# A gated linear recurrence and an ELU layer on one core: loads merged and spread over three queues, one table set for Ln and Exp, and the hand-written order replaced

## The chip, the core and the metric

The kernel runs on one core of a Trainium2 chip. A core has five engines that run side by side and meet only at semaphores: TensorE (PE; its weight loads are listed apart as PEld), VectorE (DVE), ScalarE (ACT), GpSimd (POOL) and SyncE (SP), which here only issues transfers. Each engine carries out its own list of instructions strictly in order. Transfers are issued by an engine into a queue of that engine and are then carried out by the DMA engines.

The metric is the time of one execution on the device in microseconds, the median of three runs.

## What is computed

The inputs are q, k, v, a_re and a_im of 4 batches, 8 heads, 768 steps and 48 values a head, and two weight matrices, `w_in` (384 x 2048) and `w_out` (2048 x 384), which arrive in double precision. Cut to what matters:

```python
mag = np.sqrt(a_re * a_re + a_im * a_im)
scale = np.minimum(mag, 0.999) / (mag + 1e-06)
a_re_n, a_im_n = (a_re * scale, a_im * scale)
for t in range(S):
    new_re = ar * S_re - ai * S_im
    new_im = ar * S_im + ai * S_re
    kv = np.einsum('bhd,bhe->bhde', k[:, :, t], v[:, :, t])
    S_re, S_im = (new_re + kv, new_im)
    y[:, :, t] = np.einsum('bhd,bhde->bhe', q[:, :, t], S_re)
...
h = x @ w_in
g = np.where(h > 0.0, h, alpha * (np.exp(np.minimum(h, 0.0)) - 1.0))
return g @ w_out
```

The complex gate `a` decays and turns a 48 x 48 state for each head; the outputs of the heads side by side, 3072 rows of 384, go through the two matrix products with an ELU between them.

## The kernel before

**Units.** The work is cut into 12 units (`NU`). A unit is 128 steps of two batches (`NB = 2`, function `where`): even units are batches 0 and 1, odd units batches 2 and 3, and each pair of units takes the next 128 steps. For a unit, `load` brings `ar`, `ai`, `q`, `k` and `v`, with one transfer for each of the two batches, that is 128 x 8 runs of 192 bytes, 192 KB. All go through SyncE's queue.

**One unit's steps.** Squares (`squared`, `squares`, ACT) are added (`joined`: for unit 0 on TensorE, otherwise on DVE or POOL); `logarithms` and `powers` (ACT, Ln and Exp) give the length of the gate and its inverse, `lengths`, `ratios`, `slopes` (DVE) the decay and the tangent, `angles` (ACT, arctangent) the angle. Products with triangular matrices on TensorE sum decays and angles over the steps (`sums`, `summed`, `decays`, `turned`), ACT takes exponentials (`decayed`, `quarters_used`) and sine and cosine (`waves`), DVE scales and gates q and k (`scaled`, `gated`). `noted` checks that the gate lies in the range for which this way is exact; `carry_on` keeps the last angle for the next unit of the pair. `ends` spreads the decay at chunk ends. Then the gated q and k are transposed (TensorE into PSUM, ACT copies back, L1024), `scores` and `states` are formed, `values` gives the outputs, ACT copies them out, and `seam` moves 16 rows of each head pair into place by small transfers.

**The layer.** For a unit, `inner` (L1210) forms two of 16 blocks of h, `elu` takes Relu and Exp on ACT and one `scalar_tensor_tensor` on DVE (L1221), `project` (L1235) multiplies with `w_out`. There are three PSUM buffers for `inner`, so a block waits for the `elu` of the third before. From unit 2 on the two products are cut down with sums of submatrices (`product`, L1319; `mult`, L1455), which need more additions on DVE and sums of the weights prepared once (`summed_in`, `combined`).

**Weights.** `fetch` brings one of 8 parts of `w_in` or of `w_out` (768 KB each). A part of `w_in` comes in four transfers: 48 rows into partitions 0 to 47, 48 into 64 to 111, and two of 16 rows into the gaps. `convert` rounds a part to single precision in five DVE operations, one a call (L40, L43, L46, L50, L655). Only then may `inner` or `project` use it.

**Order.** The order is written out by hand for the first 200 us or so, in the list `first`, and after that comes from `plan`: functions with a due time each, sorted. The program is issued to each engine in this order; what a transfer may overwrite is held back by semaphores. A table of activation functions is chosen with `preload_act_table_set` (`table`), and further loads stand where a function needs another set. Before, Ln comes from the set `natural_log` and Exp from `exp_and_others`; sine, cosine and arctangent from `trig_and_small`.

Lines that the prediction names: L598 load of a unit, L644 part of the weights, L705, L709, L710 squares, L716 `joined`, L731, L735, L736 logarithms, L742, L746, L747 powers, L772 lengths, L791 `noted`, L811 and L815 angles, L837 turned, L889 the first product of the decays, L920 and L904 exponentials, L951 and L954 `ends`, L973 and L977 waves, L1003 gated, L1077 to L1081 states, L1190 seam.

Of the kernel before, what the change touches and what calls it, by code (L numbers as in the profile page):

```python
# [16 lines left out]
C = 128  # L17
# [3 lines left out]
LEAST_RE = 0.7  # L21
# [484 lines left out]
def kernel(  # L506
# [12 lines left out]
    nc = tc.nc  # L519
    B, H, S, D = q.shape  # L520
# [3 lines left out]
    HD = H * D  # L524
    NB = 2
# [56 lines left out]
    def load(u, name, src, bufs, pad=False):  # L582
# [11 lines left out]
        for n in range(NB):  # L594
            to = t[:, n]
            if pad:
                to = to[:, 0:HD].rearrange("p (h d) -> p h d", h=H)
            nc.sync.dma_start(  # L598
                out=to, in_=src[b + n, :, ds(s, C)].rearrange("h p d -> p h d")
            )  # L600
        nat[u][name] = t

    def load_a(u):
        load(u, "ar", a_re, 1)
        load(u, "ai", a_im, 1)

    def load_qk(u):
        load(u, "q", q, 1)
        load(u, "k", k, 1)

    def load_v(u):
        load(u, "v", v, 2, pad=True)
# [28 lines left out]
    def fetch(kind, m):  # L641
        t, dst, pairs = weights_of(kind, m)
        for to, of in pairs:
            nc.sync.dma_start(out=to, in_=of)  # L644
        raw[kind, m] = t, dst
# [869 lines left out]
    load_a(0)  # L1515
    nc.scalar.preload_act_table_set("natural_log")
# [61 lines left out]
    def gates_of(u, *at):  # L1578
# [7 lines left out]
        (load_qk, 0), (squared, "ar", 0), (load_v, 0), (squared, "ar", 1), (squared, "ai", 0),  # L1586
        (joined, 0, 0), (squared, "ai", 1), (joined, 0, 1), (logarithms, 0, 0), (logarithms, 0, 1),
        (fetch, "in", 1), (fetch, "in", 2), (ratios, 0, 0), (lengths, 0, 0), (warm, 2), (warm, 1),
        (lengths, 0, 1), (sums, 1), *2 * [(convert,)], (table, "exp_and_others"), (ratios, 0, 1),
        (powers, 0, 0), (powers, 0, 1), (warm, 2), (sums, 0), (warm, 1), (angles, 0, 0),  # L1590
        (angles, 0, 1), (summed, 0), (summed, 1), (decayed, 0, 0), (turned, 0, 0), (decayed, 0, 1),
        (turned, 0, 1), (waves, 0, 0), (waves, 0, 1), (begun, 1), (scaled, 0, "q", 0), (warm, 1),
        (scaled, 0, "k", 1), (scaled, 0, "k", 0), (ends, 0), (scaled, 0, "q", 1), (warm, 1),
        (noted, 0), (convert,), (gated, 0, 0), (warm, 1), (warm, 2), (gated, 0, 1), (warm, 2),
        (convert,), (transposed, 0, "q", 0), (convert,), (transposed, 0, "k", 0),
# [179 lines left out]
```

## Time and profile before

| | us |
|---|---|
| median of three runs (667.33 to 667.91) | 667.35 |
| the profiled execution | 665.7 |
| its span, first to last instruction | 663.7 |
| TensorE busy | 640.6 (97%) |
| VectorE busy | 501.9 (76%) |
| ScalarE busy | 418.9 (63%) |
| GpSimd busy | 153.8 (23%) |
| L40, L43, L46, L50, L655: one operation on 128 x 768 | 0.557, 0.955, 0.556, 0.954, 0.956 |
| L1221: one operation on 128 x 512 | 0.681 |
| a table load | 1.28 |

The span is what the profile sees of one execution. Busy time is an average over stages that have different limits, so it has to be read by stretches. A matmul is listed as two instructions and its end is modelled, so a busy TensorE isn't TensorE at its peak: blocks of L1210 follow each other at 2.6 us when nothing holds them. In the chain of waits a line gives start, duration and what was under way; "issue" is time in which the engine waited for nothing that the profile shows, and "SPq" is SyncE issuing a transfer. The idle time before an instruction is put down to the semaphore that came last.

### The profile page before, as it was taken

How to read it: one execution, taken by the hardware profiler on the slowest of the kernel's cores; microseconds unless marked ns; L12 is line 12 of the kernel's file. 1: busy time of each engine (PE TensorE's matmuls, PEld its weight loads, DVE VectorE, ACT ScalarE, POOL GpSimd, SP SyncE). 2: the span in 40 equal slices, each digit the busy share in tenths (PEclk: the TensorE clock that was granted, in tenths of full speed). 3: DMA queues.
4: the chain of work that ended last, by engine and by line, in shares of the span. 5: the costliest groups of instructions: out<-in, count | busy, mean ns of one | idle time of the engine just before them, and what ended most of it. 6: DMA issues, size and time to landing. Idle time of an engine off the chain costs nothing.

```text
span 663.7 us, 17229 instructions
## 1 busy us (share of the span) xinstructions
PE 640.6 (97%) x7236; PEld 580.2 (87%) x7236; DVE 501.9 (76%) x801; ACT 418.9 (63%) x684; POOL 153.8 (23%) x200
## 2 busy tenths in 40 slices
PE   8889999999999899999999999999999999999995
PEld 6868886576897898998998998998998999999995
DVE  5798999967868689578678678678668768764481
ACT  6885367586756566767667667667677677571250
POOL 2000000112124313413403503503503502402000
PEclk9799999999999999999999999999999999999999
DMA  9997745732800713333442442451451551212100
GB/s 164 178 146 117 150 143 155 131 74 48 128 2 16 136 35 85 80 84 80 77 93 72 78 99 62 83 106 50 93 105 46 100 105 44 53 33 61 35 2 30
DMA packets 151443, 56.12 MB, mean 85 GB/s; under 512 B 129684, under 2 KB 143164, under 8 KB 151356
## 3 DMA queue, kind: packets, MB, share of 16 engines
q1 hardware_dynamic: 147616, 53.58, 39.8%
q0 software_dynamic: 3520, 1.20, 1.6%
q8 instruction: 59, 0.97, 0.6%
q14 instruction: 28, 0.23, 0.1%
q10 hardware_dynamic: 220, 0.14, 0.1%
HBM read 48.91 MB, written 4.80 MB: 81 GB/s over the span
## 4 chain that ended last, share of the span: by engine, by line
PE 63%; DVE 14%; ACT 10%; issue 5%; DMA 4%; SPq 3%; DVEq 0%; ACTq 0%
PE mlp L1319 20%; PE mlp L1455 10%; PE mlp L1210 7%; PE y L1455 5%; PE w L1023 4%; DVE g L1471 4%; PE mlp L1235 3%; PE y L1235 3%; PE y L1109 3%; DVE g L1480 3%; SPq L598 3%; DMA w<-in_moe_w_in_dram 3%; PE w L1064 2%; PE w L837 2%; ACT ee L1477 2%
## 5 line engine op out<-in xcount | busy, mean ns | idle before, releaser
L1319 PE MATMUL mlp<-w_out,g 128*128 128x192 f32 x640 | 111.8, 328 | 1.0 <-DVE ee L1331 1.0
L1319 PEld LDWEIGHTS mlp<-w_out,g 128*128 128x128 f32 x640 | 104.2, 190 | 4.4 <-DVE ee L1331 1.6
L1081 POOL TENSOR_TENSOR S<-S,T 128x384 f32<-128x384 f32 x36 | 30.2, 839 | 174.0 <-DVE S L1079 174.0
L1210 PE MATMUL mlp<-x,w_in 128*128 128x256 f32 x288 | 65.1, 384 | 0.2
L1210 PEld LDWEIGHTS mlp<-x,w_in 128*128 128x128 f32 x288 | 54.7, 193 | 9.2 <-DVE g L1221 0.7
L1471 DVE TENSOR_TENSOR g<-g,mlp 128x512 f32<-128x512 f32 x45 | 30.6, 681 | 40.1 <-ACT qt L1024 28.6
L1297 DVE TENSOR_TENSOR g<-g 128x512 f32<-128x512 f32 x80 | 54.4, 694 | 5.0 <-PE mlp L1319 3.8
L1455 PE MATMUL mlp<-x,w_in 128*128 128x128 f32 x424 | 56.2, 275 | 0.4 <-DVE o L1344 0.4
L1480 DVE SCALAR_TENSOR_TENSOR g<-ee,g 128x512 f32<-128x512 f32 x63 | 47.5, 754 | 11.1 <-ACT ee L1477 11.0
L1319 PE MATMUL mlp<-w,g 128*128 128x192 f32 x320 | 54.5, 329 | 0.0
L1319 PEld LDWEIGHTS mlp<-w,g 128*128 128x128 f32 x320 | 51.8, 190 | 0.6
L1455 PEld LDWEIGHTS mlp<-x,w_in 128*128 128x128 f32 x424 | 51.6, 192 | 0.7 <-DVE o L1344 0.6
L1190 POOL DMA_DIRECT2D x<-y x62 | 29.9, 489 | 94.8 <-ACT y L1126 43.5
L1476 ACT ACTIVATE ee<-g 128x512 f32<-128x512 f32 x63 | 39.5, 627 | 17.4 <-DVE g L1471 17.0
L1468 ACT COPY g<-mlp 128x512 f32<-128x512 f32 x36 | 21.1, 585 | 43.9 <-PE mlp L1455 43.7
L1477 ACT ACTIVATE ee<-ee 128x512 f32<-128x512 f32 x72 | 45.4, 631 | 2.3
L1024 ACT COPY qt<-w 128x512 f32<-128x512 f32 x48 | 25.8, 591 | 15.6 <-PE w L1023 15.4
L904 ACT ACTIVATE n<-w 64x384 f32<-64x384 f32 (+1 forms) x60 | 28.1, 486 | 8.9 <-PE w L889 8.3
L973 ACT ACTIVATE cs<-n 128x768 f32<-128x768 f32 (+1 forms) x14 | 10.5, 751 | 35.7 <-DVE n L845 35.6
L1455 PE MATMUL mlp<-x,g 128*128 128x128 f32 x224 | 29.7, 275 | 1.2 <-DVE o L1344 1.2
L1079 DVE TENSOR_TENSOR S<-w,S 128x384 f32<-128x384 f32 x38 | 21.0, 553 | 12.2 <-POOL S L1081 10.0
L1455 PE MATMUL y<-x,w_in 128*128 128x128 f32 x216 | 29.0, 277 | 1.2 <-ACT g L1468 1.2
(222 smaller groups left out, 1428.7 us busy)
## 6 DMA issues: line engine op xcount, KB each, us to landing
w<-in_moe_w_out_dram SPq DMA_DIRECT2D x8, 768.0 KB
g<-in_moe_w_in_dram SPq DMA_DIRECT2D x24, 256.0 KB
g<-in_moe_w_out_dram SPq DMA_DIRECT2D x24, 256.0 KB
w<-in_moe_w_in_dram SPq DMA_DIRECT2D x16, 288.0 KB
vn<-in_v_dram SPq DMA_DIRECT2D x24, 192.0 KB
ar<-in_a_re_dram SPq DMA_DIRECT2D x22, 192.0 KB
ai<-in_a_im_dram SPq DMA_DIRECT2D x22, 192.0 KB
q<-in_q_dram SPq DMA_DIRECT2D x22, 192.0 KB
```

The source lines that it names most:

```text
L904: nc.scalar.activation(out=flat(x[key][to, n : n + 1]), in_=t[of], func=AF.Exp, scale=sign)
L1081: eng.tensor_tensor(out=new_s, in0=new_s, in1=wide, op=ALU.mult)
L1190: eng.dma_start(out=x["x"][ds(j * HP + D, G), i], in_=x["y"][ds(j * HP + i * G, G)])
L1210: nc.tensor.matmul(t[:, e], lhsT=w_in[:, i, ts(f + e, C)], rhs=x["x"][:, i], start=(i == 0), stop=(i == NI - 1),)
L1235: nc.tensor.matmul(x["o", n], lhsT=x["g", f // 8][:, f % 8, ts(n, C)], rhs=w_out[:, f], start=(f == 0), stop=(f == NF - 1),)
L1297: nc.vector.tensor_tensor(out=S_of(u, k, h), in0=a, in1=b, op=op)
L1319: nc.tensor.matmul(to, lhsT=a[:, m], rhs=b[:, m], start=(first and h == 0 and m == 0), stop=False, skip_group_check=True,)
L1455: nc.tensor.matmul(x["c" + c][:, ts(m, C)], lhsT=a[:, m], rhs=x["mix"][p], start=(p == BANKS[c][0] and m == 0), stop=False, skip_group_che ...
L1471: nc.vector.tensor_tensor(out=part(u, to), in0=part(u, a), in1=part(u, b), op=op)
L1476: nc.scalar.activation(out=e, in_=part(u, of), func=AF.Relu, scale=-1.0)
L1477: nc.scalar.activation(out=e, in_=e, func=AF.Exp, scale=-1.0)
L1480: nc.vector.scalar_tensor_tensor(out=part(u, to), in0=nat[u]["e", to], scalar=-1.0, in1=part(u, of), op0=ALU.add, op1=ALU.max,)
```

## The change

- `load` brings both batches of a tensor in one transfer of 128 x 16 runs of 192 bytes, except v (its rows are padded) and unit 0's ar and ai.
- `brought` loads one tensor of a unit, by SyncE or, with `second`, by ScalarE. ScalarE issues unit 0's ai, k and q and unit 1's ar and ai.
- `fetch` gives every second transfer of a part of `w_in` to GpSimd: SyncE brings rows 0 to 47 and the first gap, GpSimd the other half. A part of `w_out` is one transfer and stays with SyncE.
- Ln and Exp both come from the set `natural_log_exp_and_others`.
- The bound of the check, `LEAST_RE`, is 0.7072 instead of 0.7.
- The list `first` is another one: unit 1's squares, logarithms and powers stand ahead of much of unit 0's states; unit 2's q and k are fetched before parts 1 and 2 of `w_in`; the check `noted` of unit 0 comes after the first half of unit 1; blocks of the layer come in another order. The plan behind the list is the same but for the name of the table.

```diff
-LEAST_RE = 0.7
+LEAST_RE = 0.7072
...
-    def load(u, name, src, bufs, pad=False):
+    def load(u, name, src, bufs, eng, pad=False):
...
-        for n in range(NB):
-            to = t[:, n]
-            if pad:
-                to = to[:, 0:HD].rearrange("p (h d) -> p h d", h=H)
-            nc.sync.dma_start(
-                out=to, in_=src[b + n, :, ds(s, C)].rearrange("h p d -> p h d")
+        if pad or u == 0 and name in ("ar", "ai"):
+            for n in range(NB):
+                to = t[:, n]
+                if pad:
+                    to = to[:, 0:HD].rearrange("p (h d) -> p h d", h=H)
+                eng.dma_start(
+                    out=to, in_=src[b + n, :, ds(s, C)].rearrange("h p d -> p h d")
+                )
+        else:
+            eng.dma_start(
+                out=t.rearrange("p n h d -> p (n h) d"),
+                in_=src[ds(b, NB), :, ds(s, C)].rearrange("n h p d -> p (n h) d"),
             )
         nat[u][name] = t
 
+    def brought(u, name, second=False):
+        src = {"ar": a_re, "ai": a_im, "q": q, "k": k, "v": v}[name]
+        load(u, name, src, 1, nc.scalar if second else nc.sync, pad=name == "v")
+
     def load_a(u):
-        load(u, "ar", a_re, 1)
-        load(u, "ai", a_im, 1)
+        brought(u, "ar")
+        brought(u, "ai")
...
-        for to, of in pairs:
-            nc.sync.dma_start(out=to, in_=of)
+        for n, (to, of) in enumerate(pairs):
+            (nc.gpsimd if n % 2 else nc.sync).dma_start(out=to, in_=of)
...
-    load_a(0)
-    nc.scalar.preload_act_table_set("natural_log")
+    brought(0, "ar")
+    brought(0, "ai", True)
+    nc.scalar.preload_act_table_set("natural_log_exp_and_others")
...
-        (load_qk, 0), (squared, "ar", 0), (load_v, 0), (squared, "ar", 1), (squared, "ai", 0),
-        (joined, 0, 0), (squared, "ai", 1), (joined, 0, 1), (logarithms, 0, 0), (logarithms, 0, 1),
-        (fetch, "in", 1), (fetch, "in", 2), (ratios, 0, 0), (lengths, 0, 0), (warm, 2), (warm, 1),
-        (lengths, 0, 1), (sums, 1), *2 * [(convert,)], (table, "exp_and_others"), (ratios, 0, 1),
...
+        (squared, "ar", 0), (squared, "ai", 0), (brought, 0, "v", False), (squared, "ar", 1),
+        (brought, 0, "k", True), (brought, 0, "q", True), (squared, "ai", 1), (joined, 0, 0),
+        (logarithms, 0, 0), (lengths, 0, 0), (joined, 0, 1), (brought, 1, "ar", True),
+        (logarithms, 0, 1), (lengths, 0, 1), (ratios, 0, 0), (ratios, 0, 1), (warm, 2), (sums, 0),
+        (sums, 1), (convert,), (powers, 0, 0), (warm, 1), (powers, 0, 1), (convert,),
+        (table, "trig_and_small", 0), (summed, 0), (angles, 0, 0), (summed, 1), (angles, 0, 1),
+        (decayed, 0, 1), (decayed, 0, 0), (turned, 0, 0), (turned, 0, 1), (brought, 1, "ai", True),
+        (waves, 0, 0), (scaled, 0, "k", 0), (begun, 1), (convert,), (waves, 0, 1),
+        (scaled, 0, "k", 1), (ends, 0), (warm, 2), (warm, 1), (warm, 1), (scaled, 0, "q", 0),
+        (load_qk, 2), (table, "natural_log_exp_and_others", 0), (scaled, 0, "q", 1), (warm, 1),
+        (gated, 0, 0), (warm, 1), (gated, 0, 1), (carry_on, 0), (fetch, "in", 1), (convert,),
+        (fetch, "in", 2), (squares, 1), (transposed, 0, "q", 0), (warm, 2), (transposed, 0, "k", 0),
+        (joined, 1), (convert,), (states, 0, 0), (logarithms, 1), (scores, 0, 0), (powers, 1),
+        (transposed, 0, "q", 1), (warm, 2), (transposed, 0, "k", 1), (ratios, 1), (lengths, 1),
+        (values, 0, 0), (slopes, 1), (scores, 0, 1), *4 * [(convert,)], (brought, 1, "q", False),
+        (decays, 1), (warm, 2), (states, 0, 1), (angles, 1), (warm, 2), (brought, 1, "k", False),
+        (values, 0, 1), (seam, 0), (fetch, "in", 3), (convert,), (turns, 1), (ends, 1), (convert,),
+        (table, "trig_and_small", 1), (noted, 1), (warm, 1), (waves, 1), (scaled, 1), (gated, 1, 0),
+        *2 * [(convert,)], (brought, 1, "v", False), (load_a, 2), (convert,), (warm, 4),
+        (inner, 0, 2), (gated, 1, 1), (fetch, "in", 4), (convert,),
+        (table, "natural_log_exp_and_others", 1), (transposed, 1, "q", 0), (transposed, 1, "k", 0),
+        (warm, 2), (states, 1, 0), (scores, 1, 0), (inner, 0, 0), (noted, 0), (load_v, 2),
+        *3 * [(convert,)], (fetch, "in", 5), (transposed, 1, "q", 1), (convert,),
+        (transposed, 1, "k", 1), (convert,), (values, 1, 0), (scores, 1, 1), (inner, 0, 4),
+        *4 * [(convert,)], (elu, 0, 2), (states, 1, 1), (convert,), (elu, 0, 0), *2 * [(convert,)],
+        (elu, 0, 4), (convert,), (values, 1, 1), (inner, 0, 6), (convert,), (inner, 0, 8),
...
-                put(r + (19.45 if u < PAIRED + 4 else 21.1), table, "exp_and_others", u)
+                put(r + (19.45 if u < PAIRED + 4 else 21.1), table, "natural_log_exp_and_others", u)
```

## The prediction

> **What bounds the kernel now.** First the busy time by stretch (stretch, length, then busy time and instruction count of PE, PEld, DVE, ACT and POOL, granted clock, DMA share, GB/s):
>
> ```profile
> 10.00:20.00 10.00, 7.21 (x54) 5.05 (x54) 6.54 (x14) 9.90 (x15) 0.64 (x1) 0.96 1.31 184
> 50.00:60.00 10.00, 10.00 (x69) 8.86 (x69) 9.63 (x13) 5.42 (x9) 0.49 (x1) 1.00 0.84 138
> 90.00:100.00 10.00, 10.00 (x48) 8.80 (x47) 9.76 (x14) 6.17 (x10) 0.00 (x0) 1.00 0.48 156
> 240.00:400.00 160.00, 158.41 (x2126) 150.80 (x2126) 122.12 (x206) 109.93 (x177) 52.48 (x57) 1.00 0.36 78
> ```
>
> Three regimes: to 25 us ScalarE's chain and the DMA engines (share over 1); from 25 to 125 us VectorE, which rounds the weights; from 75 us to the end TensorE. What remains for TensorE after about 200 us is the same list of work in both kernels, so a change there counts only where TensorE stands idle. The largest wait of TensorE between 200 and 600 us (total, times, longest):
>
> ```profile
> PE w L889 <- DVE n L772: 2.0, 8, 0.2
> ```
>
> It is 0.24 us, once a unit. The chain of waits says what is ahead of it (start, us, what):
>
> ```profile
> 298.58 1.28 ACT L735
> 299.86 0.01 issue
> 299.87 0.84 ACT n L735
> 300.71 0.73 ACT n L736
> 301.45 0.02 issue
> 301.46 0.04 ACT L746
> 301.50 1.26 issue
> 302.76 0.94 ACT n L746
> 303.70 0.02 issue
> 303.73 0.97 DVE n L772
> 304.69 0.04 issue
> 304.74 0.88 PE w L889 x8
> ```
>
> The first line is a table load for Ln (L735), the 1.26 us "issue" another for Exp (L746): 2.56 us of a chain that makes TensorE wait 0.24. At the start ACT's timeline shows the same, and the chain shows SyncE held while it issues loads:
>
> ```profile
> 9.31 0.49 ACT L731 ACTIVATE n<-w 128x384 f32<-128x384 f32 x1 [0.80 <-PE w L720]
> 9.81 1.28 ACT L1200 ACT_TABLE_LOAD   x1
> ...
> 20.09 0.60 ACT L977 ACTIVATE cs<-cs,quarter 128x384 f32<-128x384 f32 x1
> ```
>
> ```profile
> 7.45 3.90 SPq L598
> ...
> 22.14 4.38 SPq L598
> ```
>
> An issue otherwise takes 0.38 to 0.56 us. When the 3.90 ends at 11.35, SyncE had handed over 2.16 MB (ar, ai, a w_in part, q, half of k); at the 186 GB/s that the stretch 2:16 shows from 2 us on, 1.74 MB were moved. At the end of the 4.38 the sum is 4.91 against 4.41 MB. So a queue holds some 0.42 to 0.50 MB of 192-byte runs, and then the issuing engine waits.
>
> **The Trainium skill.** "ScalarE: Activation LUTs", What ACT_TABLE_LOAD costs, gives about 1283 ns for a load and as much again for a drain; the trace agrees on 1.28 and shows the chain resuming within 0.02 us, so I count 1.28. The same page, Table sets, says that natural_log_exp_and_others holds both functions. "DMA: Bandwidth & Descriptors", Issuing engines are not separate DMA queues, says that the queues of three engines run on the same 16 DMA engines and that spreading saves only issue time; the trace has one busy queue, so it cannot contradict. I share the bandwidth equally among queues.
>
> **The change, part by part.**
>
> *One table set.* From unit 3 on, Ln and Exp of a unit stand next to each other, and both loads before L735 and L746 go; each unit keeps two loads. Nine waits of 0.24 to 0.25 us (eight in 200:600, one at 199.59) end at L772, which comes up to 2.56 us earlier: 9 x 0.24 = 2.2. Bounds: nothing, if another releaser is as late; 2.2, since TensorE is otherwise busy. I take 2.1. Loads removed between 97 and 200 us lie under TensorE's products, which are busy 20.0 of 20 us there: nothing, and up to 1.28 each if that cover is gone.
>
> *ScalarE issues loads.* Before, ACT ran squares, logarithm 0, logarithm 1 (ended 9.80). Now, in order: two issues of ai, three squares, k, q, the last square, logarithm 0, unit 1's ar, logarithm 1. Each of the last three loads is a merged transfer of 2048 runs (0.39 MB). k fits. q is held until k has mostly drained, ar until q has; behind them stand the last square and logarithm 1. When ar's issue ends, ACT's queue has drained 4 x 0.39 - 0.46 = 1.11 MB; at equal shares SyncE drained about as much (ar, half a w_in part, v: 1.18) and GpSimd its 0.39: 2.68 MB. At 186 GB/s that is 14.4 us after 2.0; at 200, an estimate[...], 13.4. Taken: 15.4, then logarithm 1 ends at 15.9. If no issue is held (0.45 each) it is 11.3; at 170 GB/s 18.2.
>
> From there: lengths, the second power (+1.15), no table load (before 1.28), one load (1.28), two arctangents (0.94): +3.4, 19.3; the turns on TensorE +0.6; then VectorE's own row of turns, scaling and gating, 15.07 to 24.95 before, unchanged work 9.9. Gating of unit 0 ends at 29.8, 4.85 us later than before.
>
> *SyncE and GpSimd.* Unit 2's q and k now stand on SyncE ahead of w_in parts 1 and 2 and wait until unit 0's are gated. Their 0.79 MB, then half of part 1 (0.39), from 30 us: landed near 38, and VectorE wants part 1 at about 39.5, after unit 1's slopes. GpSimd's halves of parts 1 and 2 stand behind unit 0's carry, so from 24 us on; nothing of the seam is late for them. Part 4's half on SyncE stands behind unit 2's ar, which waits for the check of unit 0 (L791) on ACT, now put behind unit 1's first transposes: it lands about 0.5 us after VectorE wants it. The gain in issue time on SyncE is nothing by itself: it was on no engine's path but through data.
>
> *The remade list.* VectorE from the end of gating (24.87) to unit 1's last state (72.06) was 47.2 us, of which idle 1.66 + 0.79 + 0.50 + 1.15 + 0.37 = 4.5: work 42.7. The new order has, up to the same state, three rounding instructions less (L655, L40, L43: 2.3) and one less L1221 (0.6): 39.8. New idle: 0.8 behind TensorE's broadcast of the ends, 0.5 for part 4, 0.4 for others: 1.7. So 29.8 + 39.8 + 1.7 = 71.3, and unit 1's values end on TensorE near 70.8. TensorE then runs dense. Before, it had four L1210 blocks behind it at 72.2 (and lost another 0.6 up to 101); now three, so break-even is 72.2 + 0.6 - 2.6 = 70.2. Loss 0.6. In the dense stretch blocks of 2.6 us take turns with a rounding (4.0) and an L1221 (0.6) on VectorE; summed up by those rows from the last state on, the sixth and ninth L1221 come 0.2 and 0.6 us after TensorE wants their buffers, and the last part of w_out 0.9 after its product: about 1.7 in all. Before, TensorE lost 1.1 at 141 to 145, behind copies of transpositions (the new order puts products between these), beside the 0.6 already counted. Difference taken as zero, bounds -1 and +2.
>
> Sum: -2.1 + 0.6 = -1.5. The profiled execution took 665.7 us (span 663.7); against its time 664.2, against the median 667.35 **665.8 us**. The execution shown is 1.65 below the median, which I treat as the same offset in both kernels.
>
> **Rivals.**
> 1. *Slower: unit 1's ai comes late.* ACT squares it ahead of unit 0's transposition copies (L1024). It is issued after the exponentials, near 22.5, and competes with 0.79 MB of w_in from GpSimd; at 186 GB/s shared it lands between 27.5 and 32. ACT reaches it at 28.1, and each us later moves copies, scores and states, that is VectorE, by one. At 32 the sum is -1.5 + 4 = +2.5: 669.9. It decides from a landing at 31.0 on. For it: the share over 1 in 10:20, 2-KB runs against 192-byte runs; against it: GpSimd's halves may themselves wait for the carry.
> 2. *Faster: ACT isn't held*, because its queue has more room than SyncE's or drains first. Logarithm 1 then ends at 11.3, all is 4.6 us earlier: 661.2. For it: no issue by ACT was held before (0.50 us each); against it: the 3.90 and the 4.38.
> 3. *No change: the dense stretch is less well fitted*, a rounded part of w_out is late for its product by 1.5 us more: 667.3. For it: VectorE is 9.76 of 10 us busy there; against it: the work is the same.
>
> **How the numbers follow.** My sum 0.40, rival 1 0.32, rival 2 0.18, rival 3 0.10. The likeliest case alone reaches from 664 to 667.5. 0.2% (1.3 us) is about what a measurement of this kernel can tell from no change; the likeliest lies close to that edge, 0.24 of its 0.40 beyond it. Faster 0.24 + 0.18 = 0.42; same 0.16 + 0.07 + 0.01 = 0.24; slower 0.31 + 0.03 = 0.34. The range for eight in ten runs from rival 2's time to a little past rival 1's: 661 to 670.5.
>
> **What would show it.** Tables: the wait of L899 (the old L889) for VectorE gone from TensorE's waits after 200 us; if it still totals 2 us, that step is wrong. The hold: issues of q and ar by ACT of several us between 8 and 16; if they take 0.5, rival 2. The start: second half of unit 0's gating ending near 29.8, the last state of unit 1 near 71. Rival 1: ACT idle ahead of its second whole square (L720) with ai's load as releaser. Rival 3: TensorE idle between 72 and 140 us with L665 as releaser. What makes all of it wrong is a data wait on VectorE that I put at no cost: part 1 has only 1.5 us to spare.

## The result and the profile after

The changed kernel takes 671.3 us in the median (670.88 to 672.33), the kernel before 667.33 in the same session (665.58 to 667.91). The ratio is 1.0066, with a 95% interval of 1.0052 to 1.0080: slower, where the forecast said 665.8 and faster. The profiled execution took 671.3 us, its span is 669.6 (before: 665.7 and 663.7), so that the two traces differ by more (5.6 us) than the medians (4.0).

First the stretches that the prediction showed (stretch, length, then busy time and instruction count of PE, PEld, DVE, ACT and POOL, granted clock, DMA share, GB/s):

```profile
10.00:20.00 10.00, 5.50 (x13) 3.69 (x14) 3.08 (x6) 4.68 (x9) 0.00 (x0) 0.68 1.29 169
50.00:60.00 10.00, 9.74 (x126) 8.80 (x128) 9.33 (x14) 7.88 (x16) 2.02 (x4) 0.83 0.91 149
90.00:100.00 10.00, 10.00 (x48) 8.81 (x47) 9.65 (x14) 4.92 (x8) 0.00 (x0) 1.00 0.48 145
240.00:400.00 160.00, 159.18 (x1998) 152.51 (x1997) 122.62 (x206) 105.19 (x176) 49.96 (x54) 1.00 0.41 83
```

Behind 240 us TensorE is busy for 0.77 us more in 160 us than before, and its only waits from 200 to 600 us (total, times, longest) are others than the one of 2.0 us for L772:

```profile
PE mlp L1465 <- DVE o L1354: 1.7, 2, 1.2
PE y L1465 <- ACT g L1478: 1.3, 1, 1.3
PE w L1074 <- DVE S L1089: 0.4, 1, 0.4
```

Where the chain of the kernel before held two table loads, ScalarE's timeline now has the four activations (the old L735, L736, L746, L747) back to back:

```profile
257.25 0.85 ACT L745 ACTIVATE n<-ar 128x768 f32<-128x768 f32 x1
257.99 0.83 ACT L746 ACTIVATE n<-n 128x768 f32<-128x768 f32 x1
258.86 0.94 ACT L756 ACTIVATE n<-n,ln_eps 128x768 f32<-128x768 f32 x1
259.70 0.83 ACT L757 ACTIVATE n<-n 128x768 f32<-128x768 f32 x1
```

So the loss stands in the first 80 us: VectorE ends the last state of unit 1 at 77.79 us, where the kernel before has it at 72.06. VectorE is busy 3.08 us of the ten from 10 to 20 us, where it had 6.54. ScalarE's timeline shows what it did there ("ACTq" is an issue of a transfer; in brackets the idle time before and what ended it):

```profile
6.64 0.38 ACTq L603 DMA_DIRECT2D k<-in_k_dram  x1
7.05 6.82 ACTq L603 DMA_DIRECT2D q<-in_q_dram  x1
13.92 0.52 ACT L715 ACTIVATE n<-ai 128x384 f32<-128x384 f32 x1 [6.76 <-issue]
13.97 1.94 ACTq L603 DMA_DIRECT2D w<-in_a_re_dram  x1
14.35 0.47 ACT L741 ACTIVATE n<-w 128x384 f32<-128x384 f32 x1
16.18 0.49 ACT L741 ACTIVATE n<-w 128x384 f32<-128x384 f32 x1 [1.36 <-PE w L730]
```

The hold is there as forecast: k goes out in 0.38 us, q holds ScalarE for 6.82, unit 1's ar for 1.94, and the second logarithm ends at 16.67. And on VectorE, later, the last piece of gating of unit 0, the first rounding of w_in's part 4, and the last state of unit 1:

```profile
30.96 0.95 DVE L1013 TENSOR_TENSOR kg<-k,cs 128x768 f32<-128x768 f32 x1
...
72.33 0.56 DVE L40 TENSOR_SCALAR wf<-w 128x768 uint32<-128x768 uint32 x1 [4.28 <-DMA w<-in_moe_w_in_dram]
...
77.23 0.56 DVE L1091 TENSOR_TENSOR S<-S,T 128x384 f32<-128x384 f32 x1
```

VectorE, the bound from 25 to 75 us, stands still for 4.28 us because a part of the weights has not landed. SyncE's timeline says why:

```profile
60.76 0.37 SPq L603 DMA_DIRECT2D ar<-in_a_re_dram  x1
61.17 2.73 SPq L603 DMA_DIRECT2D ai<-in_a_im_dram  x1
64.00 2.52 SPq L654 DMA_DIRECT2D w<-in_moe_w_in_dram  x2
```

GpSimd had issued its half of part 4 at 51.83, and by 60 us the DMA engines had finished with it (their share is 0.06 from 58 to 60 us). SyncE's half (the third line) stands behind unit 2's ar and ai, and these wait for the check of unit 0 on ScalarE, which ends at 60.7.

### The profile page after: what moved, and what is told of

Same layout as the page of the kernel before. It is cut to its first block, busy times and chain, and to the rows that moved or that the text cites. A ratio compares the mean times of both kernels' runs of the same rounds, so it can differ in the third digit from the quotient of the medians.

```text
span 669.6 us, 17104 instructions
## 1 busy us (share of the span) xinstructions
PE 641.1 (96%) x7236; PEld 582.3 (87%) x7236; DVE 501.9 (75%) x801; ACT 392.1 (59%) x663; POOL 165.0 (25%) x216
## 4 chain that ended last, share of the span: by engine, by line
PE 50%; DVE 9%; ACT 4%; issue 2%; DMA 1%; SPq 0%; ACTq 0%; DVEq 0%
PE mlp L1329 24%; PE mlp L1465 10%; PE y L1465 5%; DVE g L1481 3%; PE w L1033 3%; DVE g L1490 3%; PE y L1119 2%; ACT ee L1487 2%; ACT ee L1486 2%; PE w L1074 2%; PE w L847 2%; DVE g L1307 1%; PE y L1110 1%; DMA ai<-in_a_im_dram 1%; PE w L899 1%
## 5 line engine op out<-in xcount | busy, mean ns | idle before, releaser
L1091 POOL TENSOR_TENSOR S<-S,T 128x384 f32<-128x384 f32 x36 | 32.1, 891 | 181.8 <-DVE S L1089 181.8
L1220 PE MATMUL mlp<-x,w_in 128*128 128x256 f32 x288 | 67.3, 393 | 0.0
L1220 PEld LDWEIGHTS mlp<-x,w_in 128*128 128x128 f32 x288 | 56.5, 199 | 8.6
L1465 PEld LDWEIGHTS mlp<-x,w_in 128*128 128x128 f32 x424 | 51.6, 192 | 0.7 <-DVE o L1354 0.6
L1229 ACT ACTIVATE ee<-mlp 128x512 f32<-128x512 f32 x24 | 14.3, 597 | 29.9 <-PE mlp L1220 21.7
```

What stands on the lines that cost most here:

```text
L1091: eng.tensor_tensor(out=new_s, in0=new_s, in1=wide, op=ALU.mult)
L1220: nc.tensor.matmul(t[:, e], lhsT=w_in[:, i, ts(f + e, C)], rhs=x["x"][:, i], start=(i == 0), stop=(i == NI - 1),)
L1465: nc.tensor.matmul(x["c" + c][:, ts(m, C)], lhsT=a[:, m], rhs=x["mix"][p], start=(p == BANKS[c][0] and m == 0), stop=False, skip_group_che ...
```

## Experiments

All medians are of several executions; the kernel before, run beside them, had medians of 667.19, 667.27, 666.79, 667.81 and 667.57. Ratios are to it, with the 95% interval; they are estimated from all executions, so that they can differ a little from the quotient of the medians. Each kernel has one trace.

| kernel | median us | ratio to before | last state of unit 1 ends (trace) |
|---|---|---|---|
| before | 667.33 | 1 | 72.06 |
| after | 671.3 | 1.0066 (1.0052 to 1.0080) | 77.79 |
| part4_first | 666.04 | 0.9982 (0.9973 to 0.9991) | 72.66 |
| no_hold | 666.65 | 0.9992 (0.9982 to 1.0002) | 71.93 |
| both | 659.96 | 0.9902 (0.9877 to 0.9928) | 67.45 |
| noted_early | 668.57 | 1.0027 (1.0016 to 1.0038) | 76.96 |
| k_only | 667.77 | 1.0012 (1.0003 to 1.0021) | 74.26 |
| before_one_set | 662.67 | 0.9933 (0.9913 to 0.9952) | 71.31 |
| before_list | 669.89 | 1.0044 (1.0029 to 1.0060) | 74.24 |
| before_halves | 669.89 | 1.0035 (1.0020 to 1.0050) | 75.40 |
| both_one_queue | 662.63 | 0.9927 (0.9903 to 0.9952) | 71.29 |
| both_two_loads | 659.55 | 0.9888 (0.9871 to 0.9904) | 67.27 |
| both_ai_sync | 660.61 | 0.9903 (0.9887 to 0.9920) | 68.94 |
| heat_both | 670.89 | 1.0058 (1.0037 to 1.0079) | 75.60 |
| heat_second | 670.12 | 1.0036 (1.0021 to 1.0052) | 77.59 |
| heat_second18 | 670.54 | 1.0055 (1.0036 to 1.0075) | 77.01 |
| heat_full | 669.93 | 1.0030 (1.0016 to 1.0044) | 77.76 |

### The two waits, each alone and both

part4_first:

```diff
-        (brought, 1, "v", False), (load_a, 2), (convert,), (warm, 4),
-        (inner, 0, 2), (gated, 1, 1), (fetch, "in", 4), (convert,),
+        (brought, 1, "v", False), (fetch, "in", 4), (convert,), (warm, 4),
+        (inner, 0, 2), (gated, 1, 1), (load_a, 2), (convert,),
```

> The kernel after with one edit: SyncE issues its half of w_in's part 4 ahead of unit 2's ar and ai, which wait for the check of unit 0. Theory 1 (the two mis-sized waits at the start add up, part 4's by 4.28 us and the held ScalarE by about 4.6 to 6): VectorE's wait of 4.28 us at 68 us is gone, the last state of unit 1 ends near 73.5, the time is 4 us below the kernel after, near 667.3, that is 1.000 of the kernel before. Theory 2 (part 4's wait only covers another one: GpSimd's half, part 5 or TensorE's blocks are as late): the wait reappears at the next part, the time stays within 1 us of 671.3, ratio 1.005 or more.

no_hold:

```diff
-        (brought, 0, "k", True), (brought, 0, "q", True), (squared, "ai", 1), (joined, 0, 0),
+        (brought, 0, "k", False), (brought, 0, "q", False), (squared, "ai", 1), (joined, 0, 0),
...
-        (logarithms, 0, 0), (lengths, 0, 0), (joined, 0, 1), (brought, 1, "ar", True),
-        (logarithms, 0, 1), (lengths, 0, 1), (ratios, 0, 0),
+        (logarithms, 0, 0), (lengths, 0, 0), (joined, 0, 1),
+        (logarithms, 0, 1), (brought, 1, "ar", True), (lengths, 0, 1), (ratios, 0, 0),
```

> The kernel after with one edit: k and q of unit 0 are issued by SyncE instead of ScalarE, and ScalarE issues unit 1's ar only behind the second logarithm. Theory 1 (ScalarE was held by its full queue): no issue by ScalarE takes over 1 us before that logarithm, which ends near 11.5 instead of 16.7; gating of unit 0 ends near 27; all that follows comes 4.6 us earlier, also the check of unit 0 and with it part 4, so VectorE's wait for part 4 stays: 666.7, ratio 0.999. Theory 2 (the loads themselves are late, whoever issues them): scaling and gating wait for k and q instead, gating ends past 30, 670 or more, ratio above 1.004.

> Both edits of part4_first and no_hold in one kernel. Theory 1 (the two waits add up): 8.5 to 9 us below the kernel after, 662.5, ratio 0.993, and the last state of unit 1 ends near 69. Theory 2 (TensorE's dense stretch behind 75 us has its own waits for VectorE, which roundings of the weights keep busy, and takes back what the start gives): no better than the better one of the two single edits, 666 to 667, ratio 0.998 to 1.000, with TensorE idle for 3 us or more between 75 and 200 us.

part4_first is 5.3 us below the kernel after, no_hold 4.65, both together 11.3. In part4_first VectorE rounds part 4 with no wait ahead of it:

```profile
66.57 0.55 DVE L40 TENSOR_SCALAR wf<-w 128x768 uint32<-128x768 uint32 x1
```

A shorter wait (1.90 us) does appear at the next part, at 76.03, where theory 2 looked for it, but it does not take the gain back. The two waits add up; neither covers the other. Not all of this is the wait itself: about 1 us of the 5.1 by which part4_first's trace reaches the last state earlier was there before the edit takes effect (gating of unit 0 ends at 30.86 instead of 31.91; the section on the clock says why). In no_hold ScalarE's timeline has the logarithms at 8.33 and 9.62 and one short issue:

```profile
8.33 0.49 ACT L741 ACTIVATE n<-w 128x384 f32<-128x384 f32 x1 [0.35 <-PE w L730]
9.62 0.49 ACT L741 ACTIVATE n<-w 128x384 f32<-128x384 f32 x1 [0.80 <-PE w L730]
9.63 0.37 ACTq L603 DMA_DIRECT2D w<-in_a_re_dram  x1
```

Gating of unit 0 ends at 25.5 instead of 31.9. SyncE is held now (k 4.06 us), but it has nothing else to do there. VectorE's wait for part 4 stays, at 4.53 us, because the whole chain up to the check has moved:

```profile
66.47 0.56 DVE L40 TENSOR_SCALAR wf<-w 128x768 uint32<-128x768 uint32 x1 [4.53 <-DMA w<-in_moe_w_in_dram]
```

With both edits VectorE's only wait of over 0.5 us between 22 and 75 us is one of 0.83, for TensorE, and this kernel is 7.2 us faster than the kernel before (6.5 by the ratio, 4.8 to 8.2 by its interval).

### What makes part 4 late, and what holds ScalarE

noted_early takes the check of unit 0 ahead of unit 1's first transposition copies and leaves SyncE's order alone:

```diff
-        (warm, 2), (states, 1, 0), (scores, 1, 0), (inner, 0, 0), (noted, 0), (load_v, 2),
+        (warm, 2), (states, 1, 0), (scores, 1, 0), (inner, 0, 0), (load_v, 2),
...
-        (table, "natural_log_exp_and_others", 1), (transposed, 1, "q", 0), (transposed, 1, "k", 0),
+        (table, "natural_log_exp_and_others", 1), (noted, 0), (transposed, 1, "q", 0), (transposed, 1, "k", 0),
```

> The kernel after with one edit: the check of unit 0 (two activations with sums) stands ahead of unit 1's first transposition copies on ScalarE instead of behind them; SyncE's order stays, with unit 2's ar and ai ahead of part 4's half. Theory 1 (that half is late because the check releases ar late): the check fits into ScalarE's idle 2.04 us there and ends 3.8 us earlier, ar is issued near 57, the half lands near 68.5, VectorE's wait for part 4 falls from 4.28 to below 1 us, 667.5, ratio 1.000. Theory 2 (it is late because 0.79 MB stand ahead of it in SyncE's queue, which fills as slowly as before while other queues share the DMA engines): the wait falls by less than half, 669.5 or more, ratio above 1.003.

SyncE's timeline shows ar released 3.85 us earlier, VectorE's the landing only 0.84 us earlier:

```profile
56.91 0.37 SPq L603 DMA_DIRECT2D ar<-in_a_re_dram  x1
57.32 2.44 SPq L603 DMA_DIRECT2D ai<-in_a_im_dram  x1
59.86 3.25 SPq L654 DMA_DIRECT2D w<-in_moe_w_in_dram  x2
```

```profile
71.49 0.56 DVE L40 TENSOR_SCALAR wf<-w 128x768 uint32<-128x768 uint32 x1 [3.39 <-DMA w<-in_moe_w_in_dram]
```

From ar's issue to the landing of part 4 it takes 14.6 us here and 11.5 in the kernel after. The trace so speaks for the second theory: most of the delay is the 0.79 MB ahead of the half in SyncE's queue, which share the DMA engines with GpSimd's half of part 5 (issued at 59.60 in the kernel after, 59.47 here); the DMA share is over 1 from 62 to 74 us in the kernel after. The median, 2.7 us below the kernel after, lies between the theories. Executions of this kernel spread from 667.06 to 671.68, and the ones in which TensorE was granted more of its clock are the shorter ones (see the section on the clock): the three at 0.983 or less took 670.6 to 671.7, the seven at 0.988 or more 667.1 to 668.4. So I take the trace for the mechanism and leave the size open.

k_only gives k of unit 0 back to ScalarE in no_hold:

```diff
-        (brought, 0, "k", False), (brought, 0, "q", False),
+        (brought, 0, "k", True), (brought, 0, "q", False),
```

> The kernel no_hold with one edit: k of unit 0 is issued by ScalarE again, q and unit 1's ar are not. Theory 1 (an issue costs its engine 0.4 us as long as the queue has room, and only what goes beyond some 0.5 MB in flight holds it): k's issue takes 0.4 us, the second logarithm ends within 0.5 us of no_hold's 10.1, the time is that of no_hold, 666.65. Theory 2 (every merged load by ScalarE at the start holds it for some microseconds): the issue takes over 2 us, 668.5 or more.

Neither theory as written. k goes out in 0.37 us and the second logarithm ends at 11.0 (10.1 in no_hold; it waited for the second half of ai), but the next issue is held:

```profile
6.34 0.37 ACTq L603 DMA_DIRECT2D k<-in_k_dram  x1
...
10.52 3.25 ACTq L603 DMA_DIRECT2D w<-in_a_re_dram  x1
13.87 1.12 ACT L752 ACTIVATE n<-n,ln_eps 128x384 f32<-128x384 f32 x2 [2.87 <-issue]
```

The same issue of ar took 0.37 us in no_hold, with k (0.39 MB) not in front of it in the queue. This is the hold by a queue's fill in its plainest form: the transfer that is issued isn't the one that costs, the next is. Whether it is bytes or the number of runs that fill a queue, these loads of 192-byte runs do not separate. Gating ends 3.0 us later than in no_hold, but only 1.1 us of this arrives in the median.

### The parts of the change on the old order

before_one_set is the kernel before with Ln and Exp from the one set, and nothing else:

```diff
-    nc.scalar.preload_act_table_set("natural_log")
+    nc.scalar.preload_act_table_set("natural_log_exp_and_others")
...
-        (lengths, 0, 1), (sums, 1), *2 * [(convert,)], (table, "exp_and_others"), (ratios, 0, 1),
+        (lengths, 0, 1), (sums, 1), *2 * [(convert,)], (ratios, 0, 1),
```

(and the same name in the two other places).

> The kernel before with one edit: Ln and Exp both come from natural_log_exp_and_others, so that the table loads between them go; order and loads stay. Theory 1 (nine waits of TensorE of 0.24 us at the first product of the decays go, the rest is covered): 2.1 us less, 665.2, ratio 0.997. Theory 2 (another releaser is as late, or the loads' time was idle time of ScalarE): within 0.5 us, ratio 0.9995 or more.

4.5 us less in the medians (3.2 to 5.8 by the interval), 2.6 between its trace and the first one of the kernel before. To see which is typical, the kernel before was profiled once more:

> The kernel before, unchanged, for a second trace of it. Theory 1 (the table set's gain of 4.5 us in the medians against 2.6 between the traces is scatter of the executions, the first trace being one of the faster ones): this execution lies near 667.3, with 1 to 2 us more in one stretch and the same waits elsewhere. Theory 2 (a gain that the first trace does not show at all): the stretches are the same within 0.3 us each.

That execution took 667.2 us, with a span of 665.3, 1.6 us more than the first trace: the last state of unit 1 comes 0.36 later, and TensorE is idle for 0.62 us more between 70 and 80 us (in part the same time) and for 0.34 more between 200 and 240. Against it the one set gains 4.2. So the first trace was one of the faster executions, as theory 1 had it. Of the gain TensorE shows 1.7 us as busy time between 240 and 600 us (0.72 and 0.96), and the last state of unit 1 comes 0.75 to 1.1 us earlier: the load between unit 0's logarithm and power also goes. The rest, 1.5 to 2 us, I can't assign.

before_list has all of the change but the order; before_halves has, of the loads, only the halves:

```diff
-        for to, of in pairs:
-            nc.sync.dma_start(out=to, in_=of)
+        for n, (to, of) in enumerate(pairs):
+            (nc.gpsimd if n % 2 else nc.sync).dma_start(out=to, in_=of)
```

> All of the change but the list: loads of both batches in one transfer, halves of w_in's parts on SyncE and GpSimd, unit 0's ai by ScalarE, one table set, with the order of the kernel before (k, q and unit 1's ar and ai by SyncE). Theory 1 (the loads' queues bring nothing by themselves, the list does, once its two waits are gone): as with the table set alone, 662.7, so 2 to 3 us behind the new list with both edits (659.96). Theory 2 (the loads bring the gain): 660 or less, the list nothing.

> The kernel before with the table set and the halves of w_in's parts on SyncE and GpSimd; order, single transfers of a batch and SyncE's loads of unit 0 stay. Theory 1 (the halves are what made the old order 7 us slower in the run with all of the change but the list: GpSimd sends its halves of parts 1 and 2 at 5 us, ahead of what the start needs, and unit 1's seam stands on GpSimd behind halves that wait for their buffer): the same loss, 668 to 670, with VectorE's wait for part 0 at 3 us or more and TensorE idle for over 2 us near 83 us. Theory 2 (the loss came from the merged loads or from ai on ScalarE): as with the table set alone, 662.7.

Both take 669.89, 7.2 us more than with the table set alone (7.4 and 6.8 by the ratios): a result that neither theory of before_list had, and that before_halves pins on the halves. The merged loads, ai on ScalarE and the new bound of the check, which only before_list has, make no difference on top of them that the scatter lets one see. VectorE's first rounding and GpSimd's timeline in before_halves:

```profile
15.04 0.56 DVE L40 TENSOR_SCALAR wf<-w 128x768 uint32<-128x768 uint32 x1 [4.64 <-DMA w<-in_moe_w_in_dram]
```

```profile
5.36 3.45 POOL L644 DMA_DIRECT2D w<-in_moe_w_in_dram  x6
...
70.38 1.09 POOL L644 DMA_DIRECT2D w<-in_moe_w_in_dram  x2 [8.30 <-DVE wp L50]
77.16 1.09 POOL L644 DMA_DIRECT2D w<-in_moe_w_in_dram  x2 [5.69 <-DVE wp L50]
78.25 1.74 POOL L1190 DMA_DIRECT2D x<-y  x3
```

In the old order GpSimd sends the halves of parts 0, 1 and 2 at once, and the rounding of part 0 waits 4.64 us (1.96 with the table set alone). That it waits for a share of the DMA engines is my reading of it: in no_hold and in the kernel with both edits, where GpSimd sends only the half of part 0 there, the wait is 2.71 and 2.35. Later GpSimd waits in line for the buffers of parts 6 and 7, and unit 1's seam stands behind: it goes out at 78.25 instead of 71.64, and TensorE is idle for 2.91 us at 84. The profile puts that wait down to L1221; that it is the seam's data is my reading, since before_one_set has 0.91 us in the same place, released by the seam's transfer.

On the new order, with both edits, the same parts were taken away one by one. both_one_queue brings every part of w_in by SyncE, both_two_loads uses one transfer per batch, both_ai_sync has unit 0's ai issued by SyncE:

```diff
-            (nc.gpsimd if n % 2 else nc.sync).dma_start(out=to, in_=of)
+            nc.sync.dma_start(out=to, in_=of)
```

```diff
-        if pad or u == 0 and name in ("ar", "ai"):
+        if True:
```

```diff
-    brought(0, "ai", True)
+    brought(0, "ai")
```

> The kernel with both edits, with all four transfers of a part of w_in on SyncE, as in the kernel before. Theory 1 (a second queue adds no bandwidth; what it brings is that GpSimd's halves of parts 1 and 2 go out while SyncE waits for unit 0's gating, and on SyncE they stand behind unit 2's q and k): part 1 lands about 2.5 us later, near 35, about when VectorE wants it, 0 to 1 us more than with two queues: 660 to 661. Theory 2 (halves on two queues are what keeps the DMA engines busy): VectorE waits several us for parts 1 and 2, 663 or more.

> The kernel with both edits, with one transfer for each batch again, as in the kernel before. Theory 1 (same runs of 192 bytes, same queue; only issue time of 0.5 us a transfer, on no engine's path): within 1 us of the kernel with both edits, 660. Theory 2 (one long transfer keeps the DMA engines fuller or is held for less long): 2 us or more slower, 662 or more.

> The kernel with both edits, with unit 0's ai issued by SyncE right behind ar, as in the kernel before. Theory 1 (a second queue brings ai no sooner, since ar and ai share the same DMA engines; ahead of part 0 on one queue it lands sooner): the second logarithm ends near 9.5 instead of 10.8, about 1 us less in all, 659. Theory 2 (part 0 then lands later and VectorE waits for it by as much): no difference, 660.

One queue costs 2.7 us in the medians (662.63 against 659.96) and 1.7 by the ratios, whose intervals overlap; that lies between the two theories and isn't clear of the scatter. Its six executions fall into two groups: three at a granted clock of 0.991 or more took 660.0 to 661.5, as theory 1 had it, three at 0.986 or less 663.8 to 665.3. Part 1 isn't what is late: it is rounded at 35.25 with no wait ahead, as theory 1 had it. What TensorE's timeline shows is a stop inside a run of equal products with no releaser, followed by half clock (see below) until 52.8 us:

```profile
38.62 0.56 PE L1110 MATMUL y<-a,vn 64*64 64x64 f32 x21
40.90 0.45 PE L1110 MATMUL y<-a,vn 64*64 64x64 f32 x11 [1.71 <-issue]
```

VectorE waits 1.91 us behind it, and the last state of unit 1 ends 3.8 us later. Whether the single queue brings such stops about or this execution (664.0 us, of the slower group) had one by chance isn't settled. The merged loads bring nothing (659.55). ai on SyncE brings nothing either (660.61): the second logarithm does end earlier, at 9.84 instead of 10.82, but VectorE then waits 3.39 us before the first rounding of part 0 instead of 2.35, as theory 2 had it (the profile names no releaser for that wait; that it is part 0's landing is my reading).

So what the halves do depends on the order. With everything on one queue the new order with both edits is as good as the old one with the table set (662.63 and 662.67). On the old order the halves cost some 7 us, on the new one they cost nothing and may gain up to 2.7, which the scatter doesn't settle.

### TensorE's clock behind an idle stretch

The granted clock is the share of its full clock that TensorE was given. In the windows behind the wait for part 4 (columns as above) it shows something that no step of the prediction had:

```profile
74.00:76.00 2.00, 0.00 (x0) 0.00 (x0) 1.97 (x4) 0.00 (x0) 0.00 (x0) 0.77 0.41 58
76.00:78.00 2.00, 1.41 (x17) 1.26 (x18) 1.86 (x5) 1.70 (x5) 0.00 (x0) 0.50 0.79 175
78.00:80.00 2.00, 2.00 (x6) 1.55 (x6) 1.97 (x4) 0.28 (x3) 1.43 (x3) 0.50 0.23 39
80.00:82.00 2.00, 2.00 (x7) 1.61 (x6) 1.97 (x4) 1.58 (x2) 1.44 (x3) 0.53 0.37 70
82.00:84.00 2.00, 2.00 (x11) 1.77 (x10) 1.86 (x3) 1.23 (x2) 0.91 (x2) 1.00 0.79 180
```

TensorE was idle from 71.7 to 76.6:

```profile
76.59 1.09 PE L1119 MATMUL y<-qt,S 128*48 128x64 f32 x16 [4.93 <-DVE S L1087]
```

When its dense products begin they run at half clock, 6 or 7 in 2 us instead of 11, until 81.9. The same happens at the start, behind the hold: idle from 9.2 to 14.5, clock 0.50 from 13.6 to 20.5. The kernel before has half clock as well (19.2 to 26.1 and 46.6 to 50.0 us), but only 10.2 us of it up to 650 us, the kernel after 20.5. The Trainium skill, "TensorE: Matmul & The Clock Gate", section "The HAM clock gate", describes it: the clock goes to half after an idle window of some 3.4 us and comes back after a busy window. The trace agrees with falls 3.4 and 4.4 us after the idle time begins and returns 5.3 and 6 us after the work resumes. It differs in that the window need not be idle throughout: the clock fell at 27.28 us too, and in the 3.41 us up to there TensorE was busy for 30%.

The traces show one thing more, and it explains a part of the scatter between executions. The clock changes only at points that lie whole multiples of 3.413 us apart, in the kernel after at 13.63, 20.45, 27.28, 30.69, 51.17, 54.58, 75.07 and 81.89. In all 18 traces a stretch of half clock lasts 3.4, 6.8 or (once, in both_one_queue) 10.2 us, save the last one, which the end of the execution cuts off. Where the points lie differs from execution to execution, so the same idle time can cost one step or two. Five traces share the kernel after's start unchanged. Its half clock ends at 17.6 us in part4_first, 18.2 in noted_early, 18.7 in heat_second, 19.2 in heat_second18 (these two are introduced below) and 20.5 in the kernel after, and gating of unit 0 ends in the same order: 30.86, 31.01, 31.21, 31.57 and 31.91.

To see what it costs, TensorE was given products of 128 x 128 that nobody reads, to fill its idle time:

```diff
+    def heat(n):
+        t = work([C, C])
+        for _ in range(n):
+            nc.tensor.matmul(t, lhsT=ident, rhs=ident, start=True, stop=True)
...
-        (logarithms, 0, 0), (lengths, 0, 0), (joined, 0, 1), (brought, 1, "ar", True),
+        (logarithms, 0, 0), (lengths, 0, 0), (heat, 11), (joined, 0, 1), (brought, 1, "ar", True),
...
-        (elu, 0, 4), (convert,), (values, 1, 1), (inner, 0, 6), (convert,), (inner, 0, 8),
+        (elu, 0, 4), (convert,), (heat, 10), (values, 1, 1), (inner, 0, 6), (convert,), (inner, 0, 8),
```

heat_both has both additions, heat_second only the second; heat_second18 has 18 there instead of 10, heat_full the 11, the 18 and 5 more ahead of unit 0's ends.

> The kernel after with 11 products of 128 x 128, which nobody reads, on TensorE ahead of the last half of unit 0's sum of squares (idle there 5.3 us) and 10 ahead of the values of unit 1's second batch (idle 4.9 us). The waits of ScalarE for its queue and of VectorE for part 4 stay. Theory 1 (TensorE's idle time brings the half clock, and that costs 1.3 us at the start and 2.1 us behind part 4): the clock stays at 1.00 in both places, gating of unit 0 ends near 30.6, twelve products of the first block behind 77 us take 2.6 us as later: 3.4 us less than the kernel after, 668. Theory 2 (the half clock comes anyway or costs nothing because VectorE is the bound there): within 1 us of 671.3, or more by the time of the products.

> The kernel after with only the 10 products ahead of the values of unit 1's second batch. Theory 1: the clock stays at 1.00 behind 75 us, 2.1 us less than the kernel after, 669.2. Theory 2: within 1 us of 671.3.

> As heat_second, with 18 products instead of 10 (4.5 us of the 4.9 us that TensorE waits). Theory 1 (the half clock costs 2.1 us behind part 4): the clock stays at 1.00 from 70 to 90 us, 669.2. Theory 2 (what the clock costs there is given back in TensorE's later waits): the clock stays at 1.00, the time is 670.5 or more, and TensorE is idle for 1 us more than in the kernel after between 90 and 240 us.

> As heat_both, with 18 products in the wait for part 4 and 5 ahead of the ends of unit 0, where the clock fell at 23.5 us. Theory 1 (start and part 4 add up): clock at 1.00 in all three places, gating near 29.8, last state of unit 1 near 75, 667.5. Theory 2 (later waits of TensorE take it back): 670 or more, with 2 us more of idle TensorE between 90 and 240 us.

In heat_both the clock stays at 1.00 up to 23.6 us and gating of unit 0 ends at 29.8, the 2.1 us earlier that the half clock and a slightly shorter hold (6.50 us) make together. Ten products took 2.5 us, too little: in heat_both and heat_second the clock fell again behind part 4, for 3.4 us each. In heat_second18 the wait is full and the clock stays:

```profile
76.00:78.00 2.00, 2.00 (x23) 1.75 (x20) 1.97 (x4) 1.28 (x5) 0.42 (x1) 1.00 0.86 186
78.00:80.00 2.00, 2.00 (x11) 1.76 (x10) 1.97 (x4) 0.84 (x2) 1.83 (x5) 1.00 0.19 49
80.00:82.00 2.00, 2.00 (x11) 1.77 (x10) 1.97 (x3) 1.97 (x5) 0.38 (x1) 1.00 0.78 168
```

That idle time brings the half clock is so shown. But the time hardly follows. By the ratios heat_both is 0.5 us below the kernel after, heat_second 2.0, heat_second18 0.7 and heat_full 2.4, where 2.1 to 3.8 were expected, and only heat_full's interval lies apart from the kernel after's (heat_second's touches it). In two of the traces TensorE's later waits take a part back: in heat_both it is idle for 0.93 us more than in the kernel after between 200 and 240 us and for 0.70 more between 400 and 600, in heat_second18 for 0.60 more between 200 and 240; in heat_second and heat_full it is not. And the idle time is not always filled: in heat_full the 11 products left 2.76 us idle at the start, and the clock fell there all the same.

What the half clock costs is therefore not settled. The products removed only a part of it: worked out from the granted clock of each execution (twice the share that is missing, times the span), the kernel after has some 23 us of half clock in the median, the four heat kernels 13 to 19, the kernel before 13 (each with 3 to 6 at its end). Within one kernel the executions with less of it are shorter (k_only: 668.4 to 669.4 us for the four at a granted clock of 0.982, 665.2 to 667.7 for the four at 0.988 or more), but stops of TensorE lengthen an execution and lower its clock both, so this alone doesn't say which brings which. As the two edits together bring 11.3 us and no filling more than 2.4, the two waits and not the clock alone are the main cause of the miss; how much of what they cost passes through the clock isn't separated.

## Why the prediction was wrong

*One table set: right.* The wait for L772 is gone (2.1 us forecast). TensorE is busy for 0.77 and 0.88 us more in 240:400 and 400:600, 1.65 of those 2.1. Alone on the old order the set is worth more, 4.5 us, since the start gains too; in my sum that load stood inside the start's chain.

*ScalarE issues loads: right in the mechanism, too small in size.* ar's issue ended at 15.91 against 15.4. That is closer than the working deserves: from 2 to 16 us the DMA engines moved 178 GB/s and not the 200 that I took, and so 2.5 MB had gone by then where I had 2.68. Logarithm 1 ended at 16.67, not 15.9, since TensorE's half clock stretched the sum of squares (1.65 us for its last two products, 0.91 in heat_both). Gating ended at 31.91, not 29.8. Of these 2.1 us 0.8 are the logarithm and 1.3 lie between the second power and the turns, where I had counted 0.6 us for TensorE: its products of the sums took 2.77 us at half clock (1.67 in the kernel with both edits), and VectorE waited 2.79 us for the turns. The step that failed here is that TensorE's clock stood in no term of the sum: at full clock (heat_both) gating ends at 29.77. How much the clock costs there is chance, though: in the four other traces with this start gating ends 0.3 to 1.05 us earlier than in the kernel after.

*SyncE and GpSimd: here the prediction failed most.* "Part 4's half on SyncE ... lands about 0.5 us after VectorE wants it": it landed 4.28 us after, a term of 0.5 us that was 3.8 too small. I had looked at what releases ar, the check on ScalarE, and not summed what is ahead of the half once ar is released: 0.79 MB in the same queue, at a rate that GpSimd's half of part 5 shares. From ar's issue at 60.76 to the landing it took 11.5 us, and releasing ar 3.85 us earlier won only 0.84. Part 1, which I named as the danger, was rounded at 41.35 with no wait ahead of it.

*The remade list: right but for what came in from outside.* From the end of gating to the last state of unit 1 I had 39.8 of work and 1.7 idle, 41.5; the trace has 45.9, and without the 3.8 us that part 4 is over its size 42.1. In the kernel with both edits it is 41.6.

*The sum.* Last state: 71.3 + 2.1 (gating) + 3.8 (part 4) + 0.6 (rest) = 77.8, measured 77.79; the rest is what was left over, so that this closes by construction. TensorE's dense stretch began at 77.61 where I had 70.8, so 6.8 late. From there to the end of the span I had 591.4 us (664.2 less the 2.0 around the span, less 70.8) and it took 592.0, although it began with 4.3 us at half clock; what made up for these isn't known. The profiled execution so ended at 664.2 + 6.8 + 0.6 less 0.3 (the time around the span, 1.7 instead of 2.0) = 671.3. My offset of 1.65 between execution and median was no property of the kernel: for the kernel after, the profiled execution is the median. Against its own execution the sum (664.2) is off by 7.1 us.

*The rivals.* Rival 1 gave 669.9, near the result, for another reason: unit 1's ai wasn't late; its squares ran at 27.82 and 28.57 without a wait. It was the right kind of event, a transfer behind others on a shared set of DMA engines, in the wrong place. Rival 2 (ScalarE isn't held, 661.2) is what the kernel became when both waits were taken away: 659.96. Of rival 3 nothing was seen; TensorE was busy 20.0 of 20 us in each of the stretches from 80 to 140. The range ended at 670.5, 0.8 below the result: it allowed for a late transfer or a held ScalarE, not for the one on top of the other. And the last line of the prediction named the right kind of fault, a data wait on VectorE put at no cost, for part 1; it came at part 4.

## What to carry to other kernels

When a transfer is moved behind another, add up the bytes ahead of it in its queue and those that other queues move meanwhile, from the moment at which the first is released, and not only the moment of release. An engine that computes on the critical path should issue only what its queue takes at once; one with nothing else to do can be held at no cost. And parts of a change that share a resource have to be tried in pairs: the same halving of the weights cost some 7 us on one order and nothing on the other.

## What the runs showed of the hardware beyond that

- An issue on ScalarE is held just as one on SyncE: 6.82 us for q behind ai and k (the kernel after), 3.25 for unit 1's ar behind ai and k (k_only), 0.37 for the same ar in no_hold, where only ai had gone before it and had landed; each is 0.39 MB. The engine computes nothing meanwhile: ScalarE is idle for 6.76 us beside the 6.82.
- Where the points at which TensorE's clock can change fall decides what an idle time does. One of 2.91 us at 81.4 us in before_halves was followed by half clock: it lies between two such points (81.1 and 84.5). One of 2.90 us at 80.2 in before_list was not: one of the points (82.1) divides it.
- TensorE stops for 0.3 to 1.7 us inside runs of products, with no releaser to be seen: 1.71 in both_one_queue, 1.41 in part4_first at 69.15, 1.31 at 37.8 in the second trace of the kernel before (0.50 in before_one_set), these three while the DMA share was over 1. The traces also list the DMA packets that bring the program's own instructions; queue q8 has 59 of them in an execution, of 16 KB each. Each of the 20 stops of 0.3 us or more ends 1.3 to 1.7 us after a packet of q8 has ended (1.66, 1.58 and 1.74 in the three), though there is only one such packet in some 11 us. So TensorE is most likely waiting for its next instructions there. What delays them isn't shown. The stops differ from execution to execution and, with the steps of the clock, are a likely part of the scatter that the kernel before itself has (665.0 to 669.5).
- One long transfer of 2048 runs of 192 bytes and two of 1024 make no difference to the time: 659.96 and 659.55.
